# Keys over means as 128 a head and 16 left over, in an attention and mixture-of-experts kernel

## The chip, the cores and the metric

The kernel runs on one core of a Trainium2 chip. The metric is the device time of one execution in microseconds. A core has five engines that run their own instruction streams and wait for each other through semaphores: TensorE (PE, matmuls and transposes), VectorE (DVE), ScalarE (ACT), GpSimd (POOL) and SyncE (SP, which here only issues transfers). 16 DMA engines move data between DRAM and the on-chip memory of 128 partitions.

## The reference

The first part is an attention over 8 batches, 8 heads, 576 positions and 64 features, in two branches that are added. The second part routes each of the 4608 tokens to one of 16 experts; the change does not touch it.

```python
q_d = q.reshape(B, H, Sd, 4, D).mean(axis=3)      # Sd = 144 means of four positions
k_d, v_d = ...                                    # the same for k and v
out_d = softmax(scale * q_d @ k_d.T) @ v_d        # 144 x 144 a head
out_up = np.repeat(out_d, 4, axis=2)              # back to 576 positions
mask = np.abs(pos[:, None] - pos[None, :]) < 4    # local branch: 7 neighbours
out_local = softmax(where(mask, scale * q @ k.T, -1e9)) @ v
attn = out_up + out_local
```

The result, as 4608 rows of 512, goes through a choice of one expert in 16 (group of 4, then 4 in the group), two matmuls of 512x1024 and 1024x512 with a ReLU between, and a weight for each token.

## The kernel before

The attention is cut into 16 units of two batches by two heads. A unit's tiles hold both heads: 64 features of each on the 128 partitions (`kt`, `qT`), or both heads side by side. The work of a unit is some forty steps, each a method of `Attention`, and the string `ORDER` lists the steps of all units in the order in which they are issued; every engine runs its own share of that list in order. A letter at the end of a step names the engine that does it (A for ACT, D for DVE, P for POOL, S for SP's queue). Steps of three to five units are interleaved. In the second half of `ORDER` the router and the first expert's work are mixed in, and after it comes the loop over the experts.

The change concerns the branch over means. Its path in one unit:

- `load_v` (lines 194 to 197) brings the positions of v into `vs`, in a layout that the host has prepared (`vm`): partition = key over means, then a chunk, then batch, then the four positions of a mean by 64 features. A head has 144 keys over means, more than the 128 partitions hold, so the 288 keys of two heads are taken in three chunks, `KEYS` (line 50): keys 0 to 111 for head 0, 176 to 287 for head 1, and a middle chunk from 112 with 64 keys, 32 of each head. Chunks 0 and 1 of `vs` are loaded over 112 partitions (448 KB), the middle one over 64 (128 KB). `vs` has three buffers, used in turn.
- `clear` with `vs` (line 126) has POOL zero partitions 64 to 111 of the middle chunk, once for each buffer.
- `pool_v` (from line 232) adds the four positions on POOL in three instructions (lines 217 to 219) and gives `vd`, 112 partitions by 3 chunks by 2 batches by 64 features, in two buffers.
- `pool_q` and `pool_k` add four positions of q and k; `s_down` (from line 309) multiplies them. A head has 144 queries too: 128 go to one PSUM tile of each head (four matmuls 64x128 by 144), and the 16 that are left, for two heads and two batches, to a tile `rest` in 32-partition strips. For head 0 such a strip is one matmul of 144 columns, for head 1 two, of 112 and 32 columns, so that its keys come in another order.
- `s_down_max`, `s_down_exp` (ACT, line 353) give `Pd`, the exponentials.
- `turn_pd` (from line 371) transposes `Pd` by PE, three transposes for each of the three key chunks, into a PSUM tile `b_pd`. `turn_pd_out` copies it to `PdT` on ACT or DVE (by `evac`, lines 166 and 168): one copy of 112x288 for chunks 0 and 2, and three copies for chunk 1 (64x256 and two of 32x64).
- `out_down` (line 406) multiplies `PdT` with `vd`: four pairs of matmuls, over 112 partitions for chunks 0 and 2, over 32 for each head's part of chunk 1.
- `out_down_out`, `turn_down`, `turn_down_out` and `down_store` bring the result in rows to DRAM (`odd`), and `load_down` reads it into `vw`, the windows of v, where the matmuls of the local branch (`x_bank`, line 446) use it.

SP's queue issues nearly all loads, in the order of `ORDER`; an issue that waits for its buffer holds all behind it. At the start it issues k and q of units 0 to 2, `vs` 0, and then k of unit 3, which needs the buffer of unit 0. POOL at the start makes the masks, clears parts of the `E` buffers (lines 118 and 119), copies four 32x32 blocks (`quarter_sum`, line 551), clears `vs` 0 and goes on with the sums of unit 1.

Of the kernel before, what the change touches and what calls it, by code (L numbers as in the profile page):

```python
# [9 lines left out]
F32 = mybir.dt.float32  # L10
# [9 lines left out]
P = 128  # L20
B, H, S, D = 8, 8, 576, 64
SD = S // 4
G = 9
# [10 lines left out]
NB = 4  # L34
# [12 lines left out]
NATURAL = 2  # L47
HALVES = (slice(0, 5), slice(5, G))

KEYS = ((slice(0, 112), 112), (slice(112, 176), 64), (slice(176, 288), 112))  # L50

TILES = (slice(0, P), slice(160, 160 + P), slice(112, 176))

# [1 line left out]
class Attention:  # L55
# [9 lines left out]
    def __init__(self, tc, q, k, vm, vw, idf, xd, left, right, dram):  # L65
        nc = self.nc = tc.nc
        self.tc, self.q, self.k, self.vm_in, self.vw_in, self.idf = tc, q, k, vm, vw, idf
        cp = self.cp = left.enter_context(tc.tile_pool(name="attc", bufs=1))
        self.a1 = left.enter_context(tc.tile_pool(name="att1", bufs=1))
        self.a2 = left.enter_context(tc.tile_pool(name="att2", bufs=2))  # L70
        self.inp = right.enter_context(tc.tile_pool(name="inp", bufs=2, side="right"))
        self.odd = [dram.tile([320, P], F32, name=f"odd{i}") for i in range(2)]
        self.st, self.banks, self.lg = {}, {}, {}
        self.turns = 0
        self.xd = xd
        self.kt = [self.inp.tile([P, 2, S], F32, name=f"kt{i}", bufs=1) for i in range(3)]
        self.kz = [self.inp.tile([P, 2, 2, S + 6], F32, name=f"kz{i}", bufs=1) for i in range(2)]
        self.load_k(0)
        self.load_q(0)
        self.mask = self.inp.tile([P, G, W], BF16, name="mask", bufs=1)  # L80
        self.vw = [(cp if i < 2 else self.inp).tile([P, 2, 2 * NBLK, D], F32, name=f"vw{i}", bufs=1) for i in range(3)]
        self.warm = self.inp.tile([P, 4 * P], BF16, name="warm", bufs=1)
        nc.vector.memset(self.warm, 0.0)
        one = cp.tile([1, 1], F32, name="one")
        nc.gpsimd.memset(one, 0.0)
        nc.scalar.activation(one, one, AF.Exp)
        self.zero = cp.tile([P, 1], F32, name="zero")
        nc.gpsimd.memset(self.zero, 0.0)
        self.idb = cp.tile([P, P], BF16, name="idb")
        self.vd = [self.inp.tile([112, 3, 2, D], F32, name=f"vd{i}", bufs=1) for i in range(2)]  # L90
        self.vs = [self.inp.tile([112, 3, 2, 4 * D], F32, name=f"vs{i}", bufs=1) for i in range(3)]
        self.mg = [cp.tile([P, 5], F32, name=f"mg{i}") for i in range(2)]
        self.sg = [cp.tile([P, 5], F32, name=f"sg{i}") for i in range(2)]
        self.rg = [cp.tile([P, 6], F32, name=f"rg{i}") for i in range(2)]
        self.kept = {}
        for n, more, shape in (
            ("pt", 1, [P, G * P]), ("x", 2, [P, G, P]), ("PdT", 1, [112, 3, 2 * SD]), ("od", 1, [P, 2 * SD]), ("odn", 1, [P, 3, 2, D])
        ):
            self.kept[n] = [cp.tile(shape, F32, name=f"{n}0")] + [self.inp.tile(shape, F32, name=f"{n}{i + 1}", bufs=1) for i in range(more)]
        self.E = [cp.tile([P, G, WW, 3], F32, name=f"E{i}") for i in range(2)]  # L100
        self.shares = self.inp.tile([P, 8], F32, name="shares", bufs=1)
        self.xT = cp.tile([P, 27 * P // 2], F32, name="xT")
        self.edge = self.inp.tile([P, 3, W], F32, name="edge", bufs=1)
# [9 lines left out]
    def clear(self, what, i):  # L113

        memset = self.nc.gpsimd.memset
        if what == "E":
            for w, c in ((slice(0, LEAD), slice(0, 3)), (slice(LEAD + W, WW), slice(0, 3)), (slice(LEAD, LEAD + W), slice(2, 3))):
                memset(self.E[i][:, :, w, c], 0.0)
            self.nc.gpsimd.tensor_copy(self.E[i][:, :, 0:40:5, 2], self.shares.unsqueeze(1).to_broadcast([P, G, 8]))
        elif what == "kz":  # L120
            memset(self.kz[i][0:64, 1], 0.0)
            memset(self.kz[i][64:P, 0], 0.0)
            for c in (slice(0, 3), slice(3 + S, 6 + S)):
                memset(self.kz[i][:, :, :, c], 0.0)
        else:
            memset(self.vs[i][64:112, 2], 0.0)

    def masks(self):

# [63 lines left out]

    def load_v(self, u):
        vs = self.vs[u % 3].rearrange("p c b x -> p c (b x)")
        self.nc.sync.dma_start(out=vs[:, 0:2], in_=self.vm_in[u, :, 0:2])
        self.nc.sync.dma_start(out=vs[0:64, 2], in_=self.vm_in[u, 0:64, 2])

    def load_windows(self, u):

# [108 lines left out]
    def s_down(self, u):  # L309

        mm = lambda *a: self.nc.tensor.matmul(*a, start=True, stop=True, skip_group_check=True)
        s = self.st[u]
        qd, kd = s["qd"], s["kd"]
        hs = (slice(0, 64), slice(64, P))
        main = [self.bank(("d", 0), u, [P, 2, SD], True)]  # L320
        both = self.bank(("d", 1), u, [P, 3, SD], True)
        main.append(both[:, 0:2])
        rest = both[:, 2]
        self.banks[("d", 1), u], self.banks[("d", 2), u] = main[1], rest
        for b in range(2):
            for h, r in enumerate(hs):
                mm(main[h][:, b], qd[r, 160 * b : 160 * b + P], kd[r, b])
        for h, r in enumerate(hs):
            for b in range(2):
                o = rest[64 * h + 32 * b : 64 * h + 32 * b + 32]  # L330
                q = qd[r, 112 + 32 * b : 144 + 32 * b]
                if h == 0:
                    mm(o, q, kd[r, b])
                else:
                    mm(o[:, 0:112], q, kd[r, b, 32:])
                    mm(o[:, 112:], q, kd[r, b, :32])

    def s_down_max(self, u):
        V = self.nc.vector
# [31 lines left out]

    def turn_pd(self, u, kc):

        pt = self.bank(("pd", kc), u, [P, 2 * SD + P])
        lo = KEYS[kc][0].start
        pd = self.st[u]["Pd"]
        tr = self.nc.tensor.transpose
        if kc == 1:
            tr(pt[:, 2 * SD :], pd[:, 4, SD - P :], self.idf)
        else:  # L380
            o = 112 - 32 * kc
            tr(pt[:112, o : o + P], pd[:, 4, 0:112], self.idf)
        for b in range(2):
            n = P if kc == 1 else 112
            tr(pt[:n, 160 * b : 160 * b + P], pd[:, 2 * b : 2 * b + 2].rearrange("p h s -> p (h s)")[:, lo : lo + n], self.idf)

    def turn_pd_out(self, u, kc, eng):
        s = self.st[u]
        s["PdT"] = self.of("PdT", u)
        pt = self.banks.pop((("pd", kc), u))  # L390
        o = s["PdT"][:, kc]
        if kc == 1:
            two = lambda x: x.rearrange("p (b s) -> p b s", b=2)[:, :, 0:P]
            self.evac(eng, two(s["PdT"][:64, kc : kc + 2].rearrange("p k s -> p (k s)")[:, 0:320]), two(pt[:64, 0:320]))
            for h in range(2):
                self.evac(eng, o[32 * h : 32 * h + 32, 112:176], pt[96:, 2 * SD + 64 * h : 2 * SD + 64 * h + 64])
        else:
            self.evac(eng, o, pt[:112, 0 : 2 * SD])

    def out_down(self, u):  # L400
        nc = self.nc
        vd, pdt = self.vd[u % 2], self.st[u]["PdT"]
        pt = self.bank("od", u, [P, 2, SD])
        for r, kc, o in ((slice(0, 112), 0, 0), (slice(0, 112), 2, 64), (slice(0, 32), 1, 0), (slice(32, 64), 1, 64)):
            for b in range(2):
                nc.tensor.matmul(
                    pt[o : o + 64, b], vd[r, (0, 2, 1)[kc], b], pdt[r, kc, SD * b : SD * b + SD], start=(kc != 1 and b == 0), stop=(kc == 1), skip_group_check=True
                )
# [807 lines left out]


ORDER = """
shared_rows; warm_up 12; masks; masks_out A; clear_windows 0; load_k 1; clear E 1; s_local 0 1; pool_q 0 D; pool_k 0 D; clear E 0; load_q 1
s_local 0 0; s_local_out 0 1; quarter_sum; clear vs 0; s_local_out 0 0; load_k 2; load_q 2; pool_q 1 P; load_v 0; s_down 0; warm_up 6  # L1220
s_down_max 0; s_local_exp 0 1; s_down_exp 0 0; s_local_exp 0 0; s_down_exp 0 2; s_down_exp 0 1; pool_q 2 D; pool_k 1 D; s_local 1 1
s_local_out 1 1; s_local 1 0; spread 2 0 A; spread 2 1 P; clear kz 0; pool_v 0; clear kz 1; clear vs 2; clear vs 1; pool_k 2 P; turn_pd 0 0
s_local_out 1 0; soft_local_sum 0 D; turn_pd 0 2; load_k 3; turn_pd 0 1; turn_pd_out 0 1 A; turn_pd_out 0 0 A; soft_local 0
turn_pd_out 0 2 A; s_down 1; s_local_exp 1 0; out_down 0; s_local_exp 1 1; turn_e 0 0; s_down_max 1; turn_e 0 2; s_down_exp 1 0
soft_down 0 D; s_down_exp 1 1; s_down_exp 1 2; clear_windows 1; load_windows 0; turn_e 0 1; out_down_out 0 D; soft_local_sum 1 D
turn_e_out 0 2 A; s_local 2 1; s_local_out 2 1; load_q 3; constants; load_k 4; s_local 2 0; spread 3 0 A; spread 3 1 P; turn_e_out 0 0 A
# [207 lines left out]
```

## Time and profile before

| | |
|---|---|
| median of 3 runs | 745.89 us (739.65 to 752.54) |
| the profiled execution | 742.23 us |
| its span, first to last instruction | 740.3 us |
| PE busy in the span | 696.6 us (94%) |
| VectorE, ScalarE, GpSimd busy | 62%, 52%, 34% |
| mean granted TensorE clock | 0.975 of full speed |

The span is that of one execution recorded by the hardware profiler. Busy times are sums over an engine's instructions; matmuls are pipelined and their recorded durations overlap, so the time from one start to the next tells more than a duration. "DMA share" is the mean busy share of the 16 DMA engines and can come out a little over 1 in a short stretch. Times in rows count from the start of the span.

### The profile page before, as it was taken

The numbers are of one execution on the slowest core, as the hardware profiler recorded it, in microseconds if no ns is written. First come the engines' busy times: TensorE is split into PE (matmuls) and PEld (weight loads), VectorE is DVE, ScalarE is ACT, GpSimd is POOL, SyncE is SP. The second block draws the span as 40 slices with busy tenths as digits, with TensorE's granted clock in tenths as the row PEclk, the third lists the DMA queues.
The fourth block names the chain that finished last, engine by engine and source line by source line (L and its number), as shares of the span: only waits on it lengthen the run. The fifth ranks groups of instructions, "written<-read, shape, count | busy, mean of one in ns | idle before, by whom it ended". The sixth has DMA issues, their size and how long they took to land. (4 is left out here: it accounts for less than half of the span.)

```text
span 740.3 us, 17944 instructions
## 1 busy us (share of the span) xinstructions
PE 696.6 (94%) x7135; PEld 627.9 (85%) x7135; DVE 460.4 (62%) x821; ACT 388.1 (52%) x830; POOL 254.8 (34%) x301
## 2 busy tenths in 40 slices
PE   7789987988986989999999999999999999999997
PEld 4666766766765868998999999999999999999996
DVE  5777987979984756654445555464555555565641
ACT  6767744857674316653444444454554554555531
POOL 7956655558634732002211120312203213212211
PEclk7889998999999999999999999999999999999999
DMA  9979899999978456846554555556655665656600
GB/s 292 250 176 238 259 265 240 237 234 272 234 212 234 114 176 207 273 131 197 156 171 143 166 188 172 191 158 204 188 172 191 212 198 189 226 186 203 222 27 26
DMA packets 109911, 144.94 MB, mean 196 GB/s; under 512 B 22736, under 2 KB 78544, under 8 KB 109824
## 3 DMA queue, kind: packets, MB, share of 16 engines
q1 hardware_dynamic: 85216, 113.25, 52.7%
q0 software_dynamic: 7088, 21.66, 8.5%
q10 hardware_dynamic: 17520, 8.85, 4.9%
q8 instruction: 57, 0.93, 0.5%
q14 instruction: 30, 0.25, 0.1%
HBM read 122.43 MB, written 22.29 MB: 195 GB/s over the span
## 5 line engine op out<-in xcount | busy, mean ns | idle before, releaser
L885 PE MATMUL ph<-xh,w1h 128*128 128x256 f32 (+13 forms) x512 | 161.1, 316 | 0.0
L856 POOL DMA_INDIRECT xg<-xd,gi x47 | 48.6, 1034 | 323.0 <-ACT yo L959 290.3
L885 PE MATMUL ph<-xl,w1h 128*128 128x256 f32 (+13 forms) x512 | 156.1, 306 | 0.0
L885 PE MATMUL ph<-xh,w1l 128*128 128x256 f32 (+13 forms) x512 | 156.0, 307 | 0.0
L844 DVE TENSOR_TENSOR w2l<-raww,w2h 128x1024 fp32r<-128x1024 f32 x61 | 74.6, 1224 | 73.7 <-ACT w2h L843 63.3
L933 PE MATMUL y<-hl,w2h 128*128 128x416 f32 (+11 forms) x384 | 115.3, 311 | 0.0
L933 PE MATMUL y<-hh,w2l 128*128 128x416 f32 (+11 forms) x384 | 114.3, 308 | 0.0
L843 ACT ACTIVATE w2h<-raww 128x1024 fp32r<-128x1024 f32 x64 | 67.6, 1058 | 73.5 <-PE y L933 54.0
L885 PEld LDWEIGHTS ph<-xh,w1h 128*128 128x128 f32 x512 | 96.2, 188 | 1.4 <-issue 0.2
L885 PEld LDWEIGHTS ph<-xl,w1h 128*128 128x128 f32 x512 | 96.3, 188 | 0.9
L844 DVE TENSOR_TENSOR w1l<-raww,w1h 128x1024 fp32r<-128x1024 f32 x60 | 73.4, 1224 | 38.1 <-ACT w1h L843 32.8
L885 PEld LDWEIGHTS ph<-xh,w1l 128*128 128x128 f32 x512 | 96.2, 188 | 0.3
L890 DVE SCALAR_TENSOR_TENSOR hl<-ph,hh 128x256 fp32r<-128x256 f32 (+13 forms) x128 | 60.3, 476 | 55.5 <-ACT hh L889 52.6
L889 ACT ACTIVATE hh<-ph 128x256 fp32r<-128x256 f32 (+13 forms) x128 | 53.9, 422 | 71.9 <-PE ph L885 65.9
L933 PE MATMUL y<-hh,w2h 128*128 128x416 f32 (+11 forms) x384 | 87.7, 312 | 0.0
L843 ACT ACTIVATE w1h<-raww 128x1024 fp32r<-128x1024 f32 x64 | 67.6, 1058 | 31.0 <-PE ph L885 24.2
L933 PEld LDWEIGHTS y<-hh,w2l 128*128 128x128 f32 x384 | 72.3, 188 | 0.1
L933 PEld LDWEIGHTS y<-hl,w2h 128*128 128x128 f32 x384 | 72.2, 188 | 0.1
L960 POOL DMA_INDIRECT out_dram<-yo,oi x47 | 47.9, 1020 | 65.5 <-ACT yo L959 51.9
L933 PEld LDWEIGHTS y<-hh,w2h 128*128 128x128 f32 x384 | 62.9, 188 | 0.1
L446 PE MATMUL b_x<-vw,pt 126*32 126x128 f32 x1152 | 40.9, 285 | 9.5 <-DMA vw<-odd 5.1
L865 ACT ACTIVATE xh<-xt 128x256 fp32r<-128x256 f32 (+14 forms) x68 | 27.0, 420 | 39.8 <-PE xt L872 39.8
(227 smaller groups left out, 1289.0 us busy)
## 6 DMA issues: line engine op xcount, KB each, us to landing
raww<-in_moe_w_dram SPq DMA_DIRECT2D x128, 512.0 KB
vw<-in_vw_dram SPq DMA_DIRECT2D x32, 378.0 KB
kt<-in_k_dram SPq DMA_DIRECT2D x16, 576.0 KB
qT<-in_q_dram SPq DMA_DIRECT2D x16, 576.0 KB
xd<-x ACTq DMA_DIRECT2D x15, 576.0 KB
vs<-in_vm_dram SPq DMA_DIRECT2D x16, 448.0 KB
vw<-odd SPq DMA_DIRECT2D x16, 144.0 KB
vs<-in_vm_dram SPq DMA_DIRECT2D x16, 128.0 KB
```

The lines of the kernel that those rows point to most:

```text
L446: self.nc.tensor.matmul(pt[32 * j : 32 * j + 32, t], self.of("pt", u)[:ROWS, 32 * lin : 32 * lin + 32], self.windows(u)[:ROWS, :, lin], st ...
L843: self.nc.scalar.activation(hi, raw, AF.Copy)
L844: eng.tensor_tensor(out=lo, in0=raw, in1=hi.bitcast(F32), op=ALU.subtract)
L856: self.nc.gpsimd.indirect_dma_start(out=xg[:w], out_offset=None, in_=self.xd[0:rows], in_offset=bass.IndirectOffsetOnAxis(ap=st["gi"][:w, ...
L865: self.nc.scalar.activation(hi, x, AF.Copy)
L885: nc.tensor.matmul(ph, a[:, k, cs], st[b][:, k], start=(n == 0), stop=(n == 11))
L889: nc.scalar.activation(hh, ph, AF.Relu)
L890: nc.vector.scalar_tensor_tensor(out=hl, in0=ph, scalar=0.0, in1=hh.bitcast(F32), op0=ALU.max, op1=ALU.subtract)
L933: nc.tensor.matmul(y, a[:, f % 2, cs], b, start=(f == 0 and n == 0), stop=(f == 7 and n == 2))
L960: i = nc.gpsimd.indirect_dma_start(out=self.out, out_offset=bass.IndirectOffsetOnAxis(ap=oi, axis=0), in_=yo[:m], in_offset=None, bounds_c ...
```

## The change

A head's 144 keys are now taken as 128 and 16 left over. Chunks 0 and 2 hold keys 0 to 127 of head 0 and 160 to 287 of the two heads' list, that is 16 to 143 of head 1; the middle chunk is a window of 128 keys from 80, of which the 32 left over (16 of each head) lie on partitions 48 to 79. `vs`, `vd` and `PdT` have 128 partitions. The host lays the main part (512 KB a unit) and the rest (64 KB) out as two contiguous blocks. The rest is loaded to partitions 48 to 79, and POOL clears all 128 partitions of the middle chunk ahead of the load, so that `out_down` can run over 64 partitions for each head with zeros in the others. `s_down` takes head 1's strips in one matmul each. `turn_pd` makes four transposes for the middle chunk.

```diff
-KEYS = ((slice(0, 112), 112), (slice(112, 176), 64), (slice(176, 288), 112))
+FIRST = (0, 80, 160)
+MAIN = P * 2 * 8 * D
...
-        self.vd = [self.inp.tile([112, 3, 2, D], F32, name=f"vd{i}", bufs=1) for i in range(2)]
-        self.vs = [self.inp.tile([112, 3, 2, 4 * D], F32, name=f"vs{i}", bufs=1) for i in range(3)]
+        self.vd = [self.inp.tile([P, 3, 2, D], F32, name=f"vd{i}", bufs=1) for i in range(2)]
+        self.vs = [self.inp.tile([P, 3, 2, 4 * D], F32, name=f"vs{i}", bufs=1) for i in range(3)]
...
-            memset(self.vs[i][64:112, 2], 0.0)
+            memset(self.vs[i][:, 2], 0.0)
...
-        self.nc.sync.dma_start(out=vs[:, 0:2], in_=self.vm_in[u, :, 0:2])
-        self.nc.sync.dma_start(out=vs[0:64, 2], in_=self.vm_in[u, 0:64, 2])
+        self.nc.sync.dma_start(out=vs[:, 0:2], in_=self.vm_in[u, 0:MAIN].rearrange("(p c x) -> p c x", p=P, c=2))
+        self.nc.sync.dma_start(out=vs[48:80, 2], in_=self.vm_in[u, MAIN:].rearrange("(p x) -> p x", p=32))
...
-                if h == 0:
-                    mm(o, q, kd[r, b])
-                else:
-                    mm(o[:, 0:112], q, kd[r, b, 32:])
-                    mm(o[:, 112:], q, kd[r, b, :32])
+                mm(o, q, kd[r, b])
...
         if kc == 1:
-            tr(pt[:, 2 * SD :], pd[:, 4, SD - P :], self.idf)
+            tr(pt[:, 224 : 224 + P], pd[:, 4, 0:P], self.idf)
+            tr(pt[:, 352 : 352 + P], pd[:, 4, SD - P :], self.idf)
         else:
             o = 112 - 32 * kc
-            tr(pt[:112, o : o + P], pd[:, 4, 0:112], self.idf)
+            tr(pt[:, o : o + P], pd[:, 4, 8 * kc : 8 * kc + P], self.idf)
...
-            self.evac(eng, two(s["PdT"][:64, kc : kc + 2].rearrange("p k s -> p (k s)")[:, 0:320]), two(pt[:64, 0:320]))
+            self.evac(eng, two(s["PdT"][:, kc : kc + 2].rearrange("p k s -> p (k s)")[:, 0:320]), two(pt[:, 0:320]))
             for h in range(2):
-                self.evac(eng, o[32 * h : 32 * h + 32, 112:176], pt[96:, 2 * SD + 64 * h : 2 * SD + 64 * h + 64])
+                self.evac(eng, o[64 * h : 64 * h + 64, 112:176], pt[64 - 64 * h : P - 64 * h, 352 - 64 * h : 416 - 64 * h])
...
-        for r, kc, o in ((slice(0, 112), 0, 0), (slice(0, 112), 2, 64), (slice(0, 32), 1, 0), (slice(32, 64), 1, 64)):
+        for r, kc, o in ((slice(0, P), 0, 0), (slice(0, P), 2, 64), (slice(0, 64), 1, 0), (slice(64, P), 1, 64)):
...
-shared_rows; warm_up 12; masks; masks_out A; clear_windows 0; load_k 1; clear E 1; s_local 0 1; pool_q 0 D; pool_k 0 D; clear E 0; load_q 1
+shared_rows; warm_up 12; masks; clear vs 0; masks_out A; clear_windows 0; load_k 1; clear E 1; s_local 0 1; pool_q 0 D; pool_k 0 D
...
-    laid["vm"] = _np.stack([mean[:, 0:112], mean[:, 176:288], mean[:, 112:224]], axis=2)
+    main = _np.stack([mean[:, 0:P], mean[:, 160:288]], axis=2)
+    laid["vm"] = _np.concatenate([x.reshape(4 * NB, -1) for x in (main, mean[:, P:160])], axis=1)
```

In `ORDER`, `clear vs 0` moves up to stand right behind `masks`, `clear vs 1` and `clear vs 2` to behind `clear E 0`, and `quarter_sum` down to the place that the two later clears had.

POOL at the start of the program, before: from the end of the masks (`edge`) to the sums of q of unit 1 (`vs_116` is `vs` 0, `E_137` and `E_136` are E 1 and E 0).

```order
L138 AFFINE_SELECT edge<-edge 128x38 x2
L118 MEMSET E_137 128x9x6 x2
L118 MEMSET E_137 128x9x38
L119 COPY E_137<-shares 128x9x8
L118 MEMSET E_136 128x9x6 x2
L118 MEMSET E_136 128x9x38
L119 COPY E_136<-shares 128x9x8
L551 COPY quarters<-idf 32x32 x4
L126 MEMSET vs_116 48x512
L217 TENSOR_TENSOR qd_346<-qT_291 128x288
```

The same place now (`vs_117` and `vs_118` are `vs` 1 and 2).

```order
L139 AFFINE_SELECT edge<-edge 128x38 x2
L127 MEMSET vs_116 128x512
L119 MEMSET E_137 128x9x6 x2
L119 MEMSET E_137 128x9x38
L120 COPY E_137<-shares 128x9x8
L119 MEMSET E_136 128x9x6 x2
L119 MEMSET E_136 128x9x38
L120 COPY E_136<-shares 128x9x8
L127 MEMSET vs_117 128x512
L127 MEMSET vs_118 128x512
L218 TENSOR_TENSOR qd_343<-qT_294 128x288
```

The quarters are gone from here, one clear stands ahead of E's and two behind; later, between the clears of `kz` 1 and the sums of k of unit 2, the quarters stand where the clears of `vs` 2 and 1 stood.

PE at `turn_pd` of unit 0 and `s_down` of unit 1, before (`b_pd` is the transposed tile, `b_d` the products of q and k over means).

```order
L379 MATMUL b_pd_0_500<-idf,Pd_376 128x128
L385 MATMUL b_pd_0_500<-idf,Pd_376 128x128 x2
L316 MATMUL b_d_1_510<-kd_385,qd_346 128x144
L316 MATMUL b_d_1_511<-kd_385,qd_346 128x144
L316 MATMUL b_d_1_510<-kd_385,qd_346 128x144
L316 MATMUL b_d_1_511<-kd_385,qd_346 128x144
L316 MATMUL b_d_1_511<-kd_385,qd_346 32x144 x2
L316 MATMUL b_d_1_511<-kd_385,qd_346 32x112
L316 MATMUL b_d_1_511<-kd_385,qd_346 32x32
L316 MATMUL b_d_1_511<-kd_385,qd_346 32x112
L316 MATMUL b_d_1_511<-kd_385,qd_346 32x32
L406 MATMUL b_od_523<-PdT_130,vd_114 64x144 x8
```

And now.

```order
L376 MATMUL b_pd_0_498<-idf,Pd_371 128x128
L377 MATMUL b_pd_0_498<-idf,Pd_371 128x128
L382 MATMUL b_pd_0_498<-idf,Pd_371 128x128 x2
L317 MATMUL b_d_1_509<-kd_380,qd_343 128x144
L317 MATMUL b_d_1_510<-kd_380,qd_343 128x144
L317 MATMUL b_d_1_509<-kd_380,qd_343 128x144
L317 MATMUL b_d_1_510<-kd_380,qd_343 128x144
L317 MATMUL b_d_1_510<-kd_380,qd_343 32x144 x4
L403 MATMUL b_od_520<-PdT_130,vd_114 64x144 x8
```

One transpose more and two matmuls fewer in a unit, in the same order. The order of transfers on SP's queue is the same; their shapes are 128x1024 and 32x512 for `vs`, and the second load of each buffer's first use waits for POOL.

## Rows read from the trace of the kernel before

**Rows 1.** The page's 40 equal slices: PE and DMA busy, in tenths.

```profile
PE   7789987988986989999999999999999999999997
...
DMA  9979899999978456846554555556655665656600
```

**Rows 2.** Busy us of each engine in three stretches, clock, DMA share, GB/s.

```profile
0.00:240.00 240.00, 205.84 (x3787) 154.03 (x3788) 187.90 (x415) 154.79 (x447) 146.20 (x204) 0.94 0.92 242
240.00:270.00 30.00, 26.56 (x182) 22.21 (x181) 24.34 (x59) 9.69 (x21) 15.33 (x7) 0.95 0.46 134
270.00:736.00 466.00, 464.19 (x3169) 451.66 (x3167) 248.15 (x349) 223.59 (x362) 92.24 (x90) 1.00 0.55 177
```

**Rows 3.** Waits from 0 to 270 us: engine, line, waited for: total, times, longest.

```profile
POOL vd L217 <- DMA vs<-in_vm_dram: 24.1, 7, 7.8
...
PE b_x L446 <- DMA vw<-odd: 5.1, 2, 2.9
...
PE xt L872 <- DMA xg<-xd,gi: 4.6, 2, 3.2
```

**Rows 4.** POOL in order of time at the start: start us, us, what [idle before].

```profile
3.97 0.72 POOL L118 MEMSET E<- 128x54 f32 x3
...
5.90 0.94 POOL L551 COPY quarters<-idf 32x32 f32<-32x32 f32 x4
6.90 0.52 POOL L126 MEMSET vs<- 48x512 f32 x1
9.55 0.69 POOL L217 TENSOR_TENSOR qd<-qT 128x288 f32<-128x288 f32 x1 [2.13 <-DMA qT<-in_q_dram]
...
16.63 1.01 POOL L217 TENSOR_TENSOR vd<-vs 112x384 f32<-112x384 f32 x1 [0.74 <-DMA vs<-in_vm_dram]
...
22.19 0.99 POOL L126 MEMSET vs<- 48x512 f32 x2
```

**Rows 5.** Groups by shape, 0 to 270 us: busy us, mean ns of one.

```profile
L406 PE MATMUL b_od<-PdT,vd 32*64 32x144 f32 x128 | 12.9, 310 | 0.4 <-ACT PdT L166 0.3
...
L406 PE MATMUL b_od<-PdT,vd 112*64 112x144 f32 x128 | 12.0, 299 | 1.9 <-DVE x L168 1.7
...
L166 ACT ACTIVATE PdT<-b_pd 112x288 f32<-112x288 f32 x26 | 10.3, 416 | 2.0 <-PE b_pd L385 1.9
...
L166 ACT ACTIVATE od<-b_od 128x288 f32<-128x288 f32 x11 | 4.6, 417 | 5.1 <-PE b_od L406 4.9
```

**Rows 6.** SP's issues of transfers at the start, in order of time.

```profile
4.29 0.59 SPq L197 DMA_DIRECT2D vs<-in_vm_dram  x1
9.07 0.35 SPq L187 DMA_DIRECT2D kt<-in_k_dram  x1
```

**Rows 7.** PE in order of time, two places late in the attention.

```profile
182.33 1.16 PE L316 MATMUL b_d<-kd,qd 64*128 64x144 f32 x20
183.42 1.36 PE L406 MATMUL b_od<-PdT,vd 112*64 112x144 f32 x16
...
189.31 0.33 PE L379 MATMUL b_pd<-idf,Pd 128*128 128x128 f32 x1
189.47 0.38 PE L385 MATMUL b_pd<-idf,Pd 128*128 128x128 f32 x2
189.69 0.27 PE L382 MATMUL b_pd<-idf,Pd 128*112 128x128 f32 x1
189.80 0.38 PE L385 MATMUL b_pd<-idf,Pd 128*112 128x128 f32 x2
```

**Rows 8.** Line 316 alone in two stretches: length, PE, PE weight loads, clock, DMA.

```profile
200.80:201.50 0.70, 0.68 (x8) 0.55 (x8) 1.00 1.12 187
201.50:201.90 0.40, 0.40 (x14) 0.35 (x12) 1.00 0.94 177
```

**Rows 9.** Two stretches at the start; the last two numbers are DMA share and GB/s.

```profile
6.00:11.00 5.00, 2.33 (x147) 1.86 (x147) 4.56 (x6) 3.24 (x1) 2.61 (x8) 1.00 1.03 414
11.00:16.60 5.60, 5.36 (x61) 2.99 (x64) 3.62 (x6) 2.63 (x11) 4.62 (x7) 0.51 1.04 267
```

More of the change, by code (lines that the diff above doesn't have):

```diff
@@ L96, in __init__ @@
         for n, more, shape in (
-            ("pt", 1, [P, G * P]), ("x", 2, [P, G, P]), ("PdT", 1, [112, 3, 2 * SD]), ("od", 1, [P, 2 * SD]), ("odn", 1, [P, 3, 2, D])
+            ("pt", 1, [P, G * P]), ("x", 2, [P, G, P]), ("PdT", 1, [P, 3, 2 * SD]), ("od", 1, [P, 2 * SD]), ("odn", 1, [P, 3, 2, D])
         ):
@@ L372, in turn_pd @@
     def turn_pd(self, u, kc):
-        pt = self.bank(("pd", kc), u, [P, 2 * SD + P])
-        lo = KEYS[kc][0].start
+        pt = self.bank(("pd", kc), u, [P, 2 * SD + 3 * 64])
+        lo = FIRST[kc]
         pd = self.st[u]["Pd"]
@@ L378, in turn_pd @@
         if kc == 1:
-            tr(pt[:, 2 * SD :], pd[:, 4, SD - P :], self.idf)
+            tr(pt[:, 224 : 224 + P], pd[:, 4, 0:P], self.idf)
+            tr(pt[:, 352 : 352 + P], pd[:, 4, SD - P :], self.idf)
         else:
             o = 112 - 32 * kc
-            tr(pt[:112, o : o + P], pd[:, 4, 0:112], self.idf)
+            tr(pt[:, o : o + P], pd[:, 4, 8 * kc : 8 * kc + P], self.idf)
         for b in range(2):
-            n = P if kc == 1 else 112
-            tr(pt[:n, 160 * b : 160 * b + P], pd[:, 2 * b : 2 * b + 2].rearrange("p h s -> p (h s)")[:, lo : lo + n], self.idf)
+            tr(pt[:, 160 * b : 160 * b + P], pd[:, 2 * b : 2 * b + 2].rearrange("p h s -> p (h s)")[:, lo : lo + P], self.idf)
     def turn_pd_out(self, u, kc, eng):
@@ L393, in turn_pd_out @@
             two = lambda x: x.rearrange("p (b s) -> p b s", b=2)[:, :, 0:P]
-            self.evac(eng, two(s["PdT"][:64, kc : kc + 2].rearrange("p k s -> p (k s)")[:, 0:320]), two(pt[:64, 0:320]))
+            self.evac(eng, two(s["PdT"][:, kc : kc + 2].rearrange("p k s -> p (k s)")[:, 0:320]), two(pt[:, 0:320]))
             for h in range(2):
-                self.evac(eng, o[32 * h : 32 * h + 32, 112:176], pt[96:, 2 * SD + 64 * h : 2 * SD + 64 * h + 64])
+                self.evac(eng, o[64 * h : 64 * h + 64, 112:176], pt[64 - 64 * h : P - 64 * h, 352 - 64 * h : 416 - 64 * h])
         else:
-            self.evac(eng, o, pt[:112, 0 : 2 * SD])
+            self.evac(eng, o, pt[:, 0 : 2 * SD])
     def out_down(self, u):
@@ L1218 @@
 ORDER = """
-shared_rows; warm_up 12; masks; masks_out A; clear_windows 0; load_k 1; clear E 1; s_local 0 1; pool_q 0 D; pool_k 0 D; clear E 0; load_q 1
[L1220 to L1223, printed above, removed]
+shared_rows; warm_up 12; masks; clear vs 0; masks_out A; clear_windows 0; load_k 1; clear E 1; s_local 0 1; pool_q 0 D; pool_k 0 D
+clear E 0; clear vs 1; clear vs 2; load_q 1; s_local 0 0; s_local_out 0 1; s_local_out 0 0; load_k 2; load_q 2; pool_q 1 P; load_v 0
+s_down 0; warm_up 6; s_down_max 0; s_local_exp 0 1; s_down_exp 0 0; s_local_exp 0 0; s_down_exp 0 2; s_down_exp 0 1; pool_q 2 D; pool_k 1 D
+s_local 1 1; s_local_out 1 1; s_local 1 0; spread 2 0 A; spread 2 1 P; clear kz 0; pool_v 0; clear kz 1; quarter_sum; pool_k 2 P
+turn_pd 0 0; s_local_out 1 0; soft_local_sum 0 D; turn_pd 0 2; load_k 3; turn_pd 0 1; turn_pd_out 0 1 A; turn_pd_out 0 0 A; soft_local 0
 turn_pd_out 0 2 A; s_down 1; s_local_exp 1 0; out_down 0; s_local_exp 1 1; turn_e 0 0; s_down_max 1; turn_e 0 2; s_down_exp 1 0
```

## The prediction

> **What bounds the kernel now.** I read the page's 40 slices first [rows 1]. They show two stages. From about the 14th slice on PE is at nine tenths or more in every slice while DMA falls to about half. Before that PE stands at seven to nine tenths and DMA at nine. The change touches only what comes before, the attention stage, so I asked next for the busy time of three stretches [rows 2]. In the first 240 us PE works 205.84 us, 86%, which leaves 34.2 us idle; the DMA engines have a mean busy share of 0.92; VectorE has 78%, ScalarE and GpSimd less. In the 466 us from 270 to 736 PE is busy for 464.19: nothing there can move unless the stage begins earlier. So attention is held by two things that are both nearly full, PE's instruction stream and the DMA engines, and a time saved at either is worth only the part that the other doesn't cover.
>
> Then the waits. GpSimd waits 24.1 us, seven times, for loads of `vs`, more than any other wait up to 270 us; but GpSimd is not the bound, and the time matters only where PE later wants `vd`. Waits of PE that a transfer ends come to 5.1 us (on the rows that go out to DRAM and back) and 4.6 us (the gathers) [rows 3]: 9.7 us beside 34.2 us of idle time, about 0.28 of it.
>
> **Start of the program, the one place where the order changes.** Before, GpSimd has its masks done near 4.0 us, clears the E buffers from 3.97, copies the quarters at 5.90, clears `vs` 0 at 6.90 in 0.52 us, and then idles 2.13 us for a load of q until 9.55 [rows 4]. Now three clears of `vs` stand in that stretch and the quarters don't: two more clears (1.04 us) against 0.94 us. The clears grow from 48 to 128 partitions with the same 512 elements; the price is 0.52 us if partitions don't count, and at most 0.82 us by E's three 128-partition clears, which take 0.72 us for 54 + 54 + 342 = 450 elements (0.72 x 512/450). Even then GpSimd is done at 3.97 + 3 x 0.82 + 1.93 (E's clears, from 3.97 to 5.90) = 8.4 us, ahead of 9.55. The 2.13 us idle hide it; without that cover it would cost 0.1 to 1 us. I take 0. Later, the two clears at 22.19 us (0.99) are replaced by the quarters (0.94): 0.
>
> The second load of `vs` 0 now waits for its clear, since both touch the same third of the tile. The clear ends near 3.97 + 0.52 = 4.5 us (4.8 at the most), and before, the load was issued at 4.29 [rows 6]: 0.2 to 0.5 us later. Behind it on SP's queue stands the load of k for unit 3, which waits for its buffer until 9.07 anyway, so nobody is held, and the transfer itself stands behind six loads of 0.59 MB. I take 0. The loads of `vs` 1 and 2 stand behind that issue at 9.07 on SP's queue, after their clears.
>
> **PE, per unit.** In `s_down` head 1 took two matmuls for each half (112 and 32 columns) and takes one of 144. Every fp32 matmul shows as two in the trace, so 20 become 16. The 20 take from 182.33 to 183.42, 1.09 us [rows 7]. Of another unit, the first eight, 128 wide, fill 0.70 us and the twelve small ones 0.40 us [rows 8]: 0.033 us each, four of them 0.13 us. Bounds: 0, if the small ones run beside each other in four places of the array and the longest chain decides; 4/20 of 1.09 us = 0.22 us if all count alike. I take the row of the small ones, 0.13 us: 16 x 0.13 = 2.1 us less (0 to 3.5).
>
> `turn_pd` gets a tenth transpose per unit. A transpose of 112 columns starts 0.11 us before the next (189.69 to 189.80), and the two of 128 columns before it last from 189.47 to 189.69, also 0.11 each [rows 7]. So widening costs nothing and one more costs 0.11 us, or 0.16 if it pays the step from the first one to the next (189.31 to 189.47). 16 x 0.11 = 1.8 us more (to 2.6). `out_down` keeps 8 matmuls of 144 columns in two halves; those over 32 partitions take 310 ns each and those over 112 take 299 [rows 5], so the number of partitions buys nothing either way: 0. The copies out of PSUM keep their lengths: ScalarE takes 416 ns over 112 partitions and 417 ns over 128 for 288 elements [rows 5]: 0. GpSimd's additions for `vd` grow in the same direction, with 384 elements as before: 0. PE together: -2.1 + 1.8 = -0.3 us (-1.7 to +2.6).
>
> **DMA, per unit.** The bytes stay: 448 + 128 KB before, 512 + 64 KB now, 0.59 MB. What changes is over how many partitions they go. The trace has a clean comparison at the start, where the engines are full throughout [rows 9]. From 6 to 11 us only loads of k and q run, 128 partitions with 4.6 KB each: 414 GB/s. From 11 to 16.6 us the queue works on `vs` 0 (112 and 64 partitions) and what follows it: 267 GB/s with the engines as busy. GpSimd gets `vs` 0 at 16.63 [rows 4].
> Before, at 267 GB/s: 0.59 MB in 2.2 us. Now 0.524 MB at 414 GB/s is 1.27 us, and the 0.066 MB over 32 partitions, at half that rate as an estimate, 0.32 us; 1.6 us in all, 0.6 us less. Bounds: 0, if the low rate belongs to the loads behind it (the value windows go to 42 partitions). On the other side, at 414 GB/s the 5.6 us would have moved 2.32 MB and moved 1.50; if all of this shortfall, 2.0 us, is `vs` 0's, it took 3.4 us and 1.8 us are saved. I take 0.6: 16 x 0.6 = 10 us of DMA time (0 to 29).
>
> How much of it reaches PE? I take the 0.28 from above, the share of PE's idle time that a transfer ends: 10 x 0.28 = 2.8 us less. Bounds: 0, if the transfers only stand earlier in the queue before a buffer that isn't free; 10 us if the DMA engines are the true bound.
>
> [...]
>
> **Sum.** -0.3 (PE) - 2.8 (DMA) + 0 (start) = -3.1 us on the profiled execution's 742.23 us: 739.1. That execution lies 3.66 us below the median of the runs, 745.89, so in the median's terms 742.8 us.
>
> **Rivals.**
> 1. The transfers' saving stays hidden. For: PE's waits for `vs` don't appear by name, the seven waits are GpSimd's [rows 3], and SP issues the next load only when a buffer is free. Against: DMA share 0.92. Time: -0.3, 745.6 us.
> 2. DMA is the bound of attention and all 10 us arrive: -10.3, 735.6 us. For: in most of the first fourteen slices it stands at nine [rows 1]. Against: PE can't give more than its 34.2 idle us, and most of its waits end on other engines.
> 3. Slower: PE's stream is the bound and the two edits don't cancel. In `s_down` the small matmuls run in four places of the array at once, the chain of head 0 (144 columns, unchanged) ends as late as head 1's two pieces, and the four instructions save nothing; the added transpose costs 0.16 us in 16 units. With the transfers hidden, +2.6: 748.5 us. It decides if the small matmuls' stretch of 0.40 us stays at 0.36 or more. For: the small ones do overlap, 14 are in flight in that stretch [rows 8]. Against: DMA gives something back.
> [...]
>
> **Chances.** Forecast 0.37, rival 1 0.25, rival 2 0.14, rival 3 0.12, rival 4 0.12. The range from 733 to 750 us takes in all five with the unknown of a few us that a shifted queue brings in a schedule written by hand; 2 in 10 are outside. About 2% (15 us) is what a measurement of this kernel can tell from no change. Below 731 needs rival 2 with more than the middle price of `vs` (its bound is 29 us): 0.07. Above 761 nothing that I can price leads: 0.04 for what I haven't seen. Within 2%: 0.89.
>
> **What would show it.** Right: the rate in the stretch after 11 us rises from 267 GB/s and GpSimd's first addition starts before 16.63; GpSimd's waits for `vs` fall below 24.1 us; `s_down`'s 16 matmuls take about 0.96 us and `turn_pd`'s ten 0.11 more; PE's busy time in attention stays within 1 us of 205.84 and its idle time falls by some 3 us. Wrong: `vs` 0 arrives no earlier (rivals 1 and 3); the start of the last stage moves by 8 us or more (rival 2); or GpSimd's q sum for unit 1 starts later than 9.55, which would mean that the clears do cost.

## The result and the profile after

| | before | after |
|---|---|---|
| median | 745.89 us (739.65 to 757.93, 13 runs) | 737.79 us (734.69 to 741.30, 13 runs) |
| profiled execution | 742.23 us | 739.77 us |
| its span | 740.3 us | 737.9 us |
| SP's transfer queue, share of the span | 52.7%, 390.1 us | 50.2%, 370.4 us |

The ratio is 0.9896, with a 95% interval from 0.9866 to 0.9926 (written [0.9866, 0.9926] from here on), so the changed kernel is faster by about 8 us of 746: under 2%, but the interval lies wholly below 1. The forecast was 742.8 us, with a range from 733 to 750: the sign is right and the time lies in the range, but the gain is more than twice the 3.1 us that the sum gave. The runs of the kernel before spread over 18 us and the ratio leaves out those over 1.5% above its fastest, so below a kernel is set against the kernel before by this ratio, and variants of the changed kernel against each other by their medians.

The two profiled executions lie 2.4 us apart, because the one of before is among its shorter ones and the one of after among its longer ones. So the traces are read for what happens in them, not for the total.

The page of after, its 40 slices, against [rows 1]:

```profile
PE   8789988989987989999999999999999999999997
...
DMA  9868899898878166746544554555646666656700
```

And the three stretches, against [rows 2] (us and instructions of each engine, clock, DMA share, GB/s):

```profile
0.00:240.00 240.00, 210.33 (x3773) 156.44 (x3775) 191.01 (x416) 156.84 (x450) 148.28 (x205) 0.94 0.86 249
240.00:270.00 30.00, 26.61 (x180) 22.77 (x179) 24.41 (x60) 8.66 (x21) 13.52 (x8) 1.00 0.33 99
270.00:736.00 466.00, 460.88 (x3137) 448.49 (x3136) 247.45 (x345) 222.67 (x361) 92.40 (x90) 1.00 0.55 176
```

The DMA share of the attention fell from 0.92 to 0.86, although 249 GB/s are moved instead of 242: more bytes in the same time with less time of the DMA engines. PE works 210.33 us of the first 240 instead of 205.84. It isn't slower; it is further on. The first matmul of the experts starts at 234.16 us where it started at 239.22, and up to there PE is busy for about as long, with less idle time. The two stretches up to that matmul, before and after:

```profile
0.00:239.20 239.20, 205.04 (x3781) 153.23 (x3782) 187.10 (x414) 154.04 (x446) 145.74 (x203) 0.94 0.92 243
...
0.00:234.10 234.10, 204.43 (x3732) 151.60 (x3734) 189.75 (x414) 154.52 (x446) 144.95 (x204) 0.94 0.86 250
```

From that matmul to the end this execution took 503.7 us against 501.1, so half of the 5.1 us is lost again. Two later traces of the changed kernel took 498.5 and 501.8 us there: a scatter of single executions, in a stage that the change doesn't touch.

The queue lines of the page (packets, MB, share of 16 engines' span), before:

```profile
q1 hardware_dynamic: 85216, 113.25, 52.7%
```

and after:

```profile
q1 hardware_dynamic: 84960, 113.25, 50.2%
```

The same bytes take 19.7 us less of the queue over the whole program. Of the first 240 us alone, before and after:

```profile
q1 hardware_dynamic: 33805, 48.17, 75.3%
...
q1 hardware_dynamic: 35514, 49.78, 69.9%
```

That is 180.7 and 167.8 us, about 13 us less for 1.6 MB more. The other 7 us of the 19.7 lie behind the attention, where no load was changed.

The start of the program, against [rows 9] (clock, DMA share and GB/s are the last three):

```profile
6.00:11.00 5.00, 3.19 (x150) 2.13 (x148) 4.56 (x6) 3.22 (x1) 2.74 (x6) 0.87 1.02 414
11.00:16.60 5.60, 5.06 (x61) 2.62 (x65) 3.74 (x6) 2.67 (x12) 5.25 (x8) 0.51 1.03 329
```

The loads of k and q run at 414 GB/s as before; the stretch with `vs` 0 rose from 267 to 329. GpSimd in order of time, against [rows 4]:

```profile
3.96 0.53 POOL L127 MEMSET vs<- 128x512 f32 x1
...
6.34 1.02 POOL L127 MEMSET vs<- 128x512 f32 x2
9.48 0.70 POOL L218 TENSOR_TENSOR qd<-qT 128x288 f32<-128x288 f32 x1 [2.12 <-DMA qT<-in_q_dram]
15.91 1.00 POOL L218 TENSOR_TENSOR vd<-vs 128x384 f32<-128x384 f32 x1
21.35 1.65 POOL L548 COPY quarters<-idf 32x32 f32<-32x32 f32 x4
```

Clears of 128 partitions take 0.51 to 0.53 us each, as the one of 48 did (0.52); the idle time ahead of 9.48 hides them all. The first addition for `vd` begins 0.72 us earlier, at 15.91.

The waits from 0 to 270 us, against [rows 3]:

```profile
POOL vd L218 <- DMA vs<-in_vm_dram: 19.0, 5, 6.2
...
PE b_x L443 <- DMA vw<-odd: 2.7, 1, 2.7
...
PE xt L869 <- DMA xg<-xd,gi: 2.0, 2, 1.3
```

All three are shorter than before (24.1, 5.1 and 4.6 us). GpSimd's sum is a weak sign: in this trace one more wait, of 10.2 us at `sl`, is put down to a load of `vs`, which `sl` doesn't read, and the two later traces of the changed kernel have 10.7 and 14.5 us for `vd`, while a kernel with a slow main load has 14.3.

PE at `s_down` and `turn_pd` of one unit, against [rows 7]:

```profile
78.30 1.14 PE L317 MATMUL b_d<-kd,qd 64*128 64x144 f32 x16
79.37 0.33 PE L376 MATMUL b_pd<-idf,Pd 128*128 128x128 f32 x1
79.53 0.27 PE L377 MATMUL b_pd<-idf,Pd 128*128 128x128 f32 x1
79.64 0.38 PE L382 MATMUL b_pd<-idf,Pd 128*128 128x128 f32 x2
```

The 16 matmuls take 1.07 us from their start to the next step's; the 20 took 1.09 [rows 7]. The added transpose takes 0.11 us (79.53 to 79.64).

### The profile page after: what moved, and what is told of

Read it like the earlier page. It is cut to its first block, busy times and chain, and to the rows that moved or that the text cites. A ratio compares the mean times of both kernels' runs of the same rounds, so it can differ in the third digit from the quotient of the medians.

```text
span 737.9 us, 17848 instructions
## 1 busy us (share of the span) xinstructions
PE 697.8 (95%) x7086; PEld 627.7 (85%) x7087; DVE 462.9 (63%) x821; ACT 388.2 (53%) x830; POOL 254.2 (34%) x301
## 3 DMA queue, kind: packets, MB, share of 16 engines
q1 hardware_dynamic: 84960, 113.25, 50.2%
## 5 line engine op out<-in xcount | busy, mean ns | idle before, releaser
L443 PE MATMUL b_x<-vw,pt 126*32 126x128 f32 x1152 | 39.2, 281 | 3.3 <-DMA vw<-odd 2.7
```

What stands on the lines that cost most here:

```text
L443: self.nc.tensor.matmul(pt[32 * j : 32 * j + 32, t], self.of("pt", u)[:ROWS, 32 * lin : 32 * lin + 32], self.windows(u)[:ROWS, :, lin], st ...
```

## The experiments

Four theories of the gain stood at the start. **A**: the loads of `vs` are faster because they go to 128 partitions, and time follows what they take of SP's queue. **B**: they are faster because the new layout in DRAM is contiguous. **C**: the gain comes from the new order of clears. **D**: it comes from PE's instructions. A fifth, **E**, came up on the way: that much of a late load's price is paid in PE's clock.

**The loads alone.** A kernel that only loads: twelve loads of a kind in a row, then a clear that waits for them all, then the next kind. Everything else of the computation is left out, and its total time means nothing.

> This kernel computes nothing of the reference: it only loads, twelve loads of one kind in a row, and clears the tile between kinds, so that each kind's rate stands by itself. Theory A (partitions): twelve main loads over 112 partitions run at 270 to 330 GB/s and those over 128 at 400 or more, whichever way the rows lie in DRAM; a pair of main and rest takes 2.2 us or more before and 1.6 us or less now. Theory B (layout in DRAM): the 112-partition load reaches 400 GB/s as soon as its source is one block, and the 128-partition load falls to about 300 GB/s with rows taken out of 6 KB. [...]

The queue in four of its stretches (29.7 to 59.8 us the main part over 112 partitions; 83 to 107.6 the new one; 205.7 to 242.6 old pairs of both loads; 265.8 to 296.5 new pairs):

```profile
q1 hardware_dynamic: 1536, 5.51, 74.1%
...
q1 hardware_dynamic: 1728, 6.29, 65.5%
...
q1 hardware_dynamic: 2496, 7.08, 79.6%
...
q1 hardware_dynamic: 2304, 7.08, 73.3%
```

Share times length, divided by twelve, is what a load takes of the DMA engines: 1.86 us for the old main part, 1.34 for the new, which holds more bytes; 2.45 us for the old pair, 1.88 for the new, 0.57 less. While they run, that is 0.459 MB in 1.86 us or 247 GB/s, against 0.524 MB in 1.34 us or 391. The first two lines also give the mean time of a packet, one piece of a transfer: 0.23 us in the first and 0.15 in the second. So the old load has fewer packets (1536 against 1728), and each takes longer. The rest, half as large now, went from 0.44 (64 partitions) to 0.24 us (32). Two cross kinds decide between A and B, by their DMA share and rate (the last two numbers) in the middle of their stretch. In order: 112 partitions out of the old, strided layout; 128 out of the new, contiguous one; 112 out of the contiguous; 128 out of the strided:

```profile
31.00:57.00 26.00, 0.00 (x0) 0.00 (x0) 1.00 0.84 209
84.00:105.00 21.00, 0.00 (x0) 0.00 (x0) 1.00 0.76 298
...
321.00:346.00 25.00, 0.00 (x0) 0.00 (x0) 1.00 0.82 218
373.00:394.00 21.00, 0.00 (x0) 0.00 (x0) 1.00 0.75 295
```

Between these two counts the number of partitions makes the rate, the layout next to nothing. The old rest loaded to partitions 48 to 111 instead of 0 to 63 took 15.8 us for twelve, where it took 15.9.

**One part alone.** Three kernels in one set with 29 runs of the kernel before. The changed kernel itself was not in this set; in the three sets that have it, its ratios are 0.9872 to 0.9903.

The kernel before with only its main load widened to 128 partitions (64 KB more a unit; the rows added are not used):

```diff
-        self.vs = [self.inp.tile([112, 3, 2, 4 * D], F32, name=f"vs{i}", bufs=1) for i in range(3)]
+        self.vs = [self.inp.tile([P, 3, 2, 4 * D], F32, name=f"vs{i}", bufs=1) for i in range(3)]
...
-    laid["vm"] = _np.stack([mean[:, 0:112], mean[:, 176:288], mean[:, 112:224]], axis=2)
+    laid["vm"] = _np.stack([mean[:, 0:128], _np.concatenate([mean[:, 176:288], mean[:, 0:16]], axis=1), mean[:, 112:240]], axis=2)
```

> The kernel before with only its main load widened to 128 partitions (64 KB more a unit, the 16 added rows not used). Theory A (partitions): the DMA queue of SP is busy less, not more, than before although it moves 1 MB more: some 15 of the 19.7 us that the change saved; the time falls by 4 to 7 us, ratio 0.991 to 0.995. Theory B (layout) and theories C (order of the clears) and D (PE's instructions): nothing is saved, the added 1 MB costs 0 to 2 us, ratio 1.000 to 1.003.

738.30 us (12 runs), ratio 0.9991 [0.9949, 1.0033]: no gain is shown, and the 0.991 to 0.995 that A expected did not come. The queue did fall, to 377.6 us. Against the next two kernels, which have both loads new, this one is 2.6 and 3.5 us longer. By itself it decides nothing.

The changed kernel with the old layout in DRAM:

```diff
-        self.nc.sync.dma_start(out=vs[:, 0:2], in_=self.vm_in[u, 0:MAIN].rearrange("(p c x) -> p c x", p=P, c=2))
...
+        self.nc.sync.dma_start(out=vs[:, 0:2], in_=self.vm_in[u, :, 0:2])
+        self.nc.sync.dma_start(out=vs[48:80, 2], in_=self.vm_in[u, 48:80, 2])
...
```

> The changed kernel with the layout in DRAM that the kernel before had (4 KB rows out of 6 KB, rest rows of 2 KB out of 6 KB). Theory A (partitions): as fast as the changed kernel, ratio 0.987 to 0.992, DMA queue of SP busy about 370 us. Theory B (layout): the gain goes, ratio 0.997 to 1.000, queue busy about 390 us.

735.73 us, ratio 0.9943 [0.9908, 0.9979], queue 372.8 us: a gain remains, and the queue is as short as A expected. The ratio is nearer to 1 than the 0.987 to 0.992 of A's forecast, so that no part of the gain is lost is not shown by this run. B's 390 us of queue did not come, and the loads alone show no effect of the layout; B falls by these two.

The changed kernel with the string `ORDER` of the kernel before:

> The changed kernel with the order of steps of the kernel before, so with the clears of vs where they were. Theory C (the order gives the gain): ratio near 1.000. Theory A: the clears of vs 1 and 2 stand at 21 to 23 us, the second load of vs 1 waits for them and holds SP's queue from 19 to 23 us; this costs 1 to 4 us of the gain, ratio 0.991 to 0.995, and before 19 us nothing differs by more than 0.5 us.

734.80 us, ratio 0.9939 [0.9897, 0.9981]: a gain without the moved clears. C falls as the cause; the kernel with slow loads below says the same from the other side.

**The loads made slow again.** Four kernels in the next set, with 17 runs of the kernel before. First the changed kernel itself:

> The changed kernel itself, so that the kernels of this set can be set against it on the same chip. Median 734 to 738 us; ratio to the kernel before 0.988 to 0.995. SP's DMA queue 368 to 373 us. If the old order of the start (734.8 us in the set before) were worth anything against the new one, this is above 737; theory C (the moved clears bring the gain) then falls the other way round, theory A expects 734 to 736.

734.83 us, ratio 0.9872 [0.9817, 0.9926]; queue 372.7 us. Then the one that weighs most, which changes only how the same values are loaded (`main` and `rest` stand for the parts of `vm`; `rest` has 32 rows of zeros more):

```diff
-        self.nc.sync.dma_start(out=vs[:, 0:2], in_=main)
-        self.nc.sync.dma_start(out=vs[48:80, 2], in_=rest)
+        self.nc.sync.dma_start(out=vs[0:112, 0:2], in_=main[0:112])
+        self.nc.sync.dma_start(out=vs[112:, 0:2], in_=main[112:])
+        self.nc.sync.dma_start(out=vs[16:80, 2], in_=rest)
```

> The changed kernel with the same bytes of main loaded as 112 partitions and 16 partitions in two loads, and the rest over 64 partitions (32 of them zero rows, so that 64 KB are added): PE, the order and the clears stay the new ones. Theory A (time follows what the loads take of SP's queue): by the loads measured alone 1.86 for 1.34 us, 0.44 for 0.24 us and something under 0.2 us for the 16, 0.72 to 0.9 us a pair, 12 to 14 us of the queue in 16 units, so 381 to 386 us of queue time; at the 0.37 us of time for each us of queue that the changed kernel gave (7.3 of 20), 4 to 5 us longer than the changed kernel: ratio to it 1.005 to 1.008. Theory D (the gain comes from PE's matmuls or the order): as the changed kernel, within 0.2%.

742.51 us (12 runs), 7.7 us above the changed kernel, more than the 4 to 5 that A expected; ratio to the kernel before 0.9987 [0.9952, 1.0021]. Queue 387.2 us. No gain is left to be seen, with PE's work, the order and the clears still new. This kernel has a third transfer and 64 KB more a unit, which the kernel before does not have; what a third transfer costs by itself was not run. Its waits from 0 to 240 us:

```profile
POOL vd L220 <- DMA vs<-in_vm_dram: 19.4, 5, 7.8
...
PE b_x L445 <- DMA vw<-odd: 4.9, 4, 2.4
```

PE's wait for the rows that come back from DRAM is 4.9 us, as before the change (5.1). The eight traces of kernels without a slow load of `vs` (the one below with loads left out among them) have 1.4 to 2.8; with one slow load it is 3.7 (only main widened) and 3.3 (only main slow). These rows are no part of `vs`; that they come late because the queue ahead of them is longer fits, but is argued.

The other direction, without 13 of the 16 main loads (values of an earlier unit are used instead, so the output is another):

```diff
-        self.nc.sync.dma_start(out=vs[:, 0:2], in_=main)
+        if u < 3:
+            self.nc.sync.dma_start(out=vs[:, 0:2], in_=main)
```

> The changed kernel with the main load left out for all units from the fourth on (the values of an earlier unit are used instead, so the output is another): 13 loads of 1.34 us, 17 us less of SP's queue. Theory A with an even price: 353 us of queue and 6 us (0.37 of 17) less time, ratio to the changed kernel 0.991 to 0.993. Theory A with a price that fades as the queue empties: 0.996 to 1.000. Theory D: within 0.2% of it.

730.31 us, 4.5 less than the changed kernel, with 350.6 us of queue (22 less). The direction is A's, but the price is lower here: 0.26 us of time for each of the 17.4 us that 13 loads take alone. That lies between the 6 us that A expected at an even price and the 3 us or less at one that fades as the queue empties.

PE's part undone alone, `s_down`'s strips of head 1 in two matmuls of 112 and 32 columns again:

```diff
-                mm(o, q, kd[r, b])
+                if h == 0:
+                    mm(o, q, kd[r, b])
+                else:
+                    mm(o[:, 0:112], q, kd[r, b, :112])
+                    mm(o[:, 112:], q, kd[r, b, 112:])
```

> The changed kernel with the four strips of the second head in eight matmuls of 112 and 32 columns again. By the prediction's step (0.13 us a unit in 16 units) 2.1 us longer, ratio to the changed kernel 1.003, and the stretch of s_down back from 1.07 us or below. By what the trace of the changed kernel shows (1.09 us for 20 matmuls, 1.07 us for 16) 0.3 us, ratio 1.000, stretch 1.07 to 1.10 us.

733.90 us, 0.9 below the changed kernel, which six runs of each (731.31 to 738.49 and 732.68 to 737.48) don't tell from none. The merged matmuls save nothing that can be seen. With the slow loads, where all of PE's new work gained nothing, D falls.

**The main load alone, and the clock.** A last set, with 33 runs of the kernel before.

> The changed kernel once more, as the anchor of this set: 734 to 738 us, 8 to 9 us below the kernel before.

738.53 us, ratio 0.9903 [0.9871, 0.9935].

The main load split as above, the rest left new:

> The changed kernel with its main load split into 112 and 16 partitions, the rest as in the changed kernel and no byte added. By the loads alone 0.52 us for the main part and up to 0.2 for the second transfer, 8 to 11.5 us of queue in 16 units: 379 to 384 us. Theory A at 0.4 to 0.55 us of time for a us of queue: 3.5 to 6 us longer than the changed kernel, ratio to it 1.005 to 1.008. If it was the rest's load (64 KB less, half the partitions) that made the gain: within 0.2% of the changed kernel.

742.58 us, 4.0 above the changed kernel, ratio to the kernel before 0.9960 [0.9925, 0.9994]: the main part carries about half, and with the 7.7 of both loads in the set before the rest carries something like the other half. The two come from different sets, and here too a transfer is added, so the division is rough.

For theory E, the kernel with slow loads and the changed kernel got eight empty matmuls at each of two places (parts of two lines of `ORDER`):

```diff
-load_v 4; out_down 2
+load_v 4; warm_up 8; out_down 2
...
-x_bank_out 5 2 A; s_local 9 0
+x_bank_out 5 2 A; warm_up 8; s_local 9 0
```

> The kernel with slow loads (7.7 us longer than the changed kernel) with eight empty matmuls of 512 columns ahead of each of two places where PE stands idle for 2 us or more in most traces (near 42 and near 112 us) and after which the granted clock was 0.50 for up to 8 us. Theory E (half or more of the loads' price is paid in the clock that falls behind a wait): the stretch behind each place keeps a clock of 0.9 or more, and 3 to 6 us come back. Theory A alone (only waiting counts): no gain, within 0.3%, or 0.5 to 1 us longer by the empty matmuls.

> The changed kernel with the same empty matmuls at the same two places. Theory E: 1.5 to 4 us shorter than the changed kernel, because its clock falls there in some executions and not in others (one of its two traces shows 1.00 from 44 to 52 us, the other 0.50 to 0.88); its mean granted clock rises from 0.980 by 0.002 to 0.005. Theory A alone: within 0.3% of the changed kernel, or 0.5 to 1 us longer.

747.87 us with slow loads, ratio to the kernel before 1.0019 [0.9984, 1.0054], where the unfilled one had 0.9987 in the other set; and 740.47 us for the changed kernel, 1.9 longer than unfilled, ratio 0.9930 [0.9896, 0.9964] against 0.9903. The intervals overlap, so neither is shown to be longer; neither is shorter, which is what E expected. The first place did what it was meant to. Before it was filled, the slow-load kernel's stretch there reads (clock, DMA share and GB/s last):

```profile
44.00:48.00 4.00, 2.35 (x36) 1.82 (x36) 3.26 (x5) 1.72 (x5) 2.96 (x3) 0.75 0.67 178
48.00:52.00 4.00, 4.00 (x47) 2.55 (x39) 1.17 (x3) 0.49 (x1) 0.00 (x0) 0.50 0.70 216
```

and filled:

```profile
44.00:48.00 4.00, 3.78 (x58) 2.43 (x60) 3.90 (x7) 2.50 (x6) 3.43 (x3) 1.00 0.84 229
48.00:52.00 4.00, 4.00 (x78) 3.23 (x68) 3.13 (x8) 1.47 (x7) 0.00 (x0) 1.00 0.70 215
```

The clock stays at 1.00 and PE does 78 matmuls instead of 47 in the second four microseconds; `s_down` starts there at 48.49 us instead of 50.79. Yet the kernel is not shorter. At the second place the empty matmuls had to wait themselves, here in the changed kernel:

```profile
110.95 2.46 PE L157 MATMUL warmps<-warm 128*128 128x512 bf16 x8 [2.45 <-ACT x L167]
```

They wait for ScalarE, which reads `x` out of PSUM late; with slow loads the wait there is 2.25 us. So this place can add a wait of its own. E is not supported, and not refuted cleanly either. Against it: the mean granted clock over all runs of the slow-load kernel rose from 0.974 to 0.980 by the filling, the changed kernel's value, and no time came back; and over the first 240 us the traces have 0.94 before, 0.94 with slow loads, and 0.94, 0.94 and 0.95 after. For it: over whole runs the clock goes with the loads, 0.972 to 0.974 before and 0.978 to 0.980 after, though it is 0.978 with the slow main load too. That a part of the gain is clock is left open.

## Why the prediction was right or wrong

**The transfers' own time: right.** The step gave 0.6 us a pair and 10 us in 16 units. Alone, a pair takes 0.57 us less, 9.2 us in 16 units; both of its times are longer than the step's (2.45 and 1.88 us for 2.2 and 1.6), and the difference holds. Inside the kernel SP's queue gains about 13 us in the attention. The rest was priced at half the rate of main, 0.32 us; no row shows that half, and alone the rest takes 0.24 us. Rival 4, 0.12 of the chances, had main take the same time over 112 as over 128 partitions; it takes 1.86 against 1.34 us, so this rival falls. Moving the old rest from partitions 0 to 63 to 48 to 111 changed next to nothing (15.9 and 15.8 us for twelve).

**How much of it reaches PE: wrong, and the failed step.** The prediction multiplied by 0.28, "the share of PE's idle time that a transfer ends". Measured, about half to all of the loads' own time arrives: by the ratios 7.2 to 9.5 us of 9.2 in the three sets that hold both kernels; 7.7 us for slow loads that alone cost 11.5 (0.72 in 16 units) and a small third transfer; 4.0 for a main part that alone costs 8.3 and that transfer. The share was also taken over two stretches, waits up to 270 us by idle time up to 240; over the first 240 us for both it is 9.2 of 34.2 us, 0.27, so that is not the cause.

The 0.28 counts a wait of PE as the transfer's only where the transfer is the last link. One place in the trace of before shows the links ahead of it:

```profile
108.21 1.00 POOL L217 TENSOR_TENSOR vd<-vs 112x384 f32<-112x384 f32 x1 [7.84 <-DMA vs<-in_vm_dram]
...
116.27 0.49 ACT L166 ACTIVATE x<-b_x 128x384 f32<-128x384 f32 x1 [4.08 <-DMA xd<-x]
...
118.18 0.48 PE L265 MATMUL b_s<-mask,idb 128*128 128x380 bf16 x1 [3.68 <-ACT Pd L353]
```

PE's 3.68 us stand under ScalarE's name. But ScalarE had itself stood still for 4.08 us until 116.27, for the store of an earlier `x`, a transfer, with a DMA share of 0.94 while ScalarE waited; its exponentials `Pd`, queued behind, came late. So such chains exist, and the 0.28 leaves them out. That they make the difference is not shown: ScalarE's waits for transfers from 0 to 240 us come to 12.7 us before and to 11.3, 6.5 and 10.8 in the traces of after, but to 14.3 in each of the two kernels with new loads and the old order or the old layout. By which path the rest of the saved time reaches PE stays open.

The prediction also says that GpSimd "is not the bound, and the time matters only where PE later wants `vd`". GpSimd's additions hold what is queued behind them, at 108.21 the sums of q and k, which start at 111.32 and 115.76 us, and a copy for the local branch at 114.53. Whether that cost PE time was not tested.

Where attention ends parts the kernels, with one trace for each time. The start of the last `out_down` group and of the first expert matmul:

| kernel | last `out_down`, us | first expert matmul, us |
|---|---|---|
| 13 main loads left out | 204.90 | 227.98 |
| after with the old order | 208.37 | 230.93 |
| after with the old layout | 210.53 | 233.71 |
| after with split `s_down` | 211.82 | 233.70 |
| after, its three traces | 211.42, 213.36, 212.76 | 234.16, 236.59, 236.49 |
| after with empty matmuls | 212.36 | 237.38 |
| before with main over 128 | 213.18 | 237.85 |
| slow loads | 215.88 | 238.95 |
| before | 216.22 | 239.22 |
| slow main load | 217.60 | 242.28 |
| slow loads with empty matmuls | 220.02 | 244.15 |

Every trace with a main load over 128 partitions lies ahead of every one with a load over 112. Kernels with the same loads lie up to 6.5 us apart, so the order within the two groups says little; the trace of the slow main load is its longest execution (745.86 us).

Rival 2, the DMA engines as the bound of attention with all 10 us arriving (735.6 us), came nearer than the forecast. Its objection, that PE has only 34.2 idle us to give, was no objection: 8 us fit. But its sign, a last stage that starts 8 us or more earlier, is not met: 2.6 to 5.1 us in the three traces. That a smaller share arrives when 13 main loads are left out (0.26) fits a bound that passes to something else soon after; what that is stays open.

**PE: one term mis-sized.** `s_down` was to save 0.13 us a unit, by the rate of the small matmuls' busy time [rows 8]. It saves 0.02. With the first eight at 0.70 us, as read there, the small ones keep 0.37 of their 0.40 us, so rival 3's condition (0.36 or more) was met. Its reason, that the small ones run in four places at once and head 0's strips of 144 columns end as late as head 1's two pieces, fits and is argued; four places at once are not shown, only that the small ones overlap, twelve of 0.19 us or more each in 0.40 us in the trace of before. The transpose costs the 0.11 us that was forecast. PE's stream got 16 x (0.11 - 0.02) = 1.4 us longer, not 0.3 shorter. That this is not seen in the end is in line with a bound that is not PE's stream. Two signs on PE were no use: its busy time up to 240 us was to stay within 1 us of 205.84 and is 210.33, 207.26 and 204.79 us in the three traces of after, and its idle time was to fall by 3 us from 34.2 and is 29.7, 32.7 and 35.2. The copies out of PSUM kept their length, 416 ns for 288 elements over 128 partitions as over 112, and `out_down` its 1.3 us.

**The start: right.** The clears cost nothing, the q sums begin at 9.48 instead of 9.55, and the old order on the changed kernel is not slower. One detail was off: the quarters, in their new place, take 1.65 instead of 0.94 us, with no consequence.

**The range** held the time, 5 us below the forecast, because it reached down to rival 2's price for the case of a full bound; that is its width, not the sum.

## What to carry to other kernels

Where the DMA engines stand at nine tenths for a whole stage, as here at 0.92, don't price a saved microsecond of transfer by the share of PE's waits that name a transfer: here that share was 0.28, and about half to all of the loads' own time arrived, a quarter where 13 loads fell away. Follow each long wait of PE one or two links back, to what the engine that released it had waited for. Look at each load's rate while it runs alone: here a load over 112 partitions cost 1.4 times one over 128 that brought more bytes (1.86 and 1.34 us). In this kernel, small matmuls whose times overlapped saved 0.02 us a unit when they were merged (1.09 and 1.07 us), and nothing that could be seen in the time.

## What was not expected

The size of the difference between 112 and 128 partitions, 247 against 391 GB/s at rows of 4 KB in both, and that the DRAM layout had next to no part in it (209 and 218 GB/s over 112 partitions, 298 and 295 over 128). Why a packet of the load over 112 partitions takes longer stays open; no run here tells. Also that a stretch at half the clock (0.50 from 48 to 52 us, 1.00 when filled) could be removed without any gain in time that could be seen; where the 2.3 us went by which `s_down` started earlier there is not shown.
